# Top-32 attention with an MLP behind it: masks as a parametric ReLU on ScalarE, the mean taken from x by GpSimd, the first eight units turned one step sooner

## The chip, the cores and the metric

The kernel runs on one core of one Trainium2 chip. The metric is the device time of one execution in microseconds (us); less is better. The engines are called as in the profile: PE (TensorE matmul), PEld (its weight loads), DVE (VectorE), ACT (ScalarE), POOL (GpSimd), SP (SyncE, which issues DMAs). All arithmetic is float32.

## What is computed

```python
# q, k, v: (8, 8, 576, 64)      w_ch1: (512, 2048)   w_ch2: (2048, 512)   g_ln: (512,)
scores = q @ k.transpose(0, 1, 3, 2) / sqrt(64)
kth    = the 32nd largest of each row
scores = where(scores >= kth, scores, -1e9)
attn   = softmax(scores)                       # denominator + 1e-9
x      = (attn @ v), heads side by side        # (8, 576, 512)

mu, var = mean and variance of each row of x
xn  = (x - mu) / sqrt(var + 1e-6) * g_ln
out = x + relu(xn @ w_ch1) @ w_ch2
```

`1 / sqrt(var + 1e-6)` is positive, so it can be applied after the ReLU and the second product, and the kernel does so. Both weights come as float64 and are turned to float32 on the chip, piece by piece (32 pieces of 128 x 512).

## The kernel before

The work is cut into 160 **units**: for a batch `b` and a pair of heads `hp`, one tile of 128 query rows (two heads, so two score tiles of 128 x 576), or the **rest** of 64 rows of both heads (one tile of 128 x 576). Batch 0 has units 0 to 7 (query tiles 0 and 1 of the four pairs), 8 to 15 (tiles 2 and 3) and 16 to 19 (the rests). Units of one job form a **group**, for which the product with v is made at once. When the fourth pair of a group of tiles is done, the rows of x are complete, and a **block** of 2 or 3 tiles of 128 rows goes to the MLP.

One step `n` of the main loop works on several units at once: scores of unit n+1, selection of the 32 largest of unit n, mask of unit n-1, exponential and transposition of unit n-2, product with v of the group that ended at n-3.

```python
def select(u, i):                       # four rounds, i = 0..3
    nt = range(len(u.tiles))
    ...
    for t in nt:
        nc.vector.max(m[:, t, :], u.cur[t])            # the 8 largest
    if i < TOP_K // 8 - 1:
        for t in nt:
            ...
            nc.vector.match_replace(u.wk[t][:], m[:, t, :], u.cur[t], LOWEST)
    ...
    u.thr = m                           # thr[:, t, 7] is the 32nd largest

def prepare(u):
    ...
    if u.shared:                        # units 0..15, beside the weights
        ...
        nc.scalar.activation(u.e[:, 0], u.sc[:, 0], AF.Sign, bias=u.less[:])
        nc.scalar.activation(u.e[:, 0], u.e[:, 0], AF.Relu, scale=MASKED)
    else:
        nc.gpsimd.tensor_scalar_mul(u.bias[:, 0:nt], u.top[:, 0:nt, 0], -scale)

def mask(u, t):
    e, sc = u.e[:, t], u.sc[:, t]
    if u.shared and t == 0:
        nc.gpsimd.tensor_tensor(e, sc, e, ALU.subtract)
    else:
        nc.gpsimd.tensor_scalar(e, sc, u.thr[:, t, 7:8], MASKED, ALU.is_lt, ALU.mult)
        nc.gpsimd.tensor_tensor(e, e, sc, ALU.add)
```

A weight piece goes through `fetch` (DMA), `split` (three ACT ops and a clamp on POOL), `shift` (DVE) and `join` (two POOL ops), spread over three steps. Before, two pieces are split in each of the steps 0 to 15. The first weight is centred, so that the mean of a row of x falls out of the product: each column has g times the weight, less the mean of that over the 512 rows.

```python
def mean_of(nb):                        # 4 matmuls for each quarter of w_ch1
    means[nb] = product("mean")
    for c in range(NC):
        nc.tensor.matmul(means[nb][:], gmat[0][:, c], w1[:, c, nb * DM : (nb + 1) * DM], ...)

def centre(nb):                         # 4 DVE ops for each quarter
    for c in range(NC):
        w = w1[:, c, nb * DM : (nb + 1) * DM]
        nc.vector.scalar_tensor_tensor(out=w, in0=w, scalar=gcol[:, c : c + 1],
                                       in1=means[nb][:], op0=ALU.mult, op1=ALU.subtract)
    centred[nb] = now[0]
```

The MLP of a block is a list of small items for PE (`todo`): transposition of x (0.44), then 64 `hidden` matmuls (0.44 for two tiles, 0.66 for three) and 16 `project` matmuls for each tile (0.875). These are the kernel's own constants in us. In each step `fill` is called eight times; each call adds a share to `owed` and takes items while they are paid for. `DVE_UNIT, DVE_REST = 10.3, 5.3`, and `pe_cost` adds what PE does for attention in that step: 1.5 for scores (1.25 for a rest), 1.0 for transpositions (0.67), 3.0 when a group's product is due.

```python
def fill():
    owed[0] = min(owed[0] + share[0], 6.0)
    while todo and owed[0] >= todo[0][1] / 2 and (not todo[0][3] or todo[0][3]()):
        pop()

def slot(n):
    if not all(map(done, ready)):       # weights not all turned yet
        return 1.2
    return max(0.0, dve_cost(n) - pe_cost(n)) / SLOTS
```

What is left in `todo` when the loop ends runs on PE at the end. A `hidden` item may run only when its quarter of `w_ch1` is done, a `project` item when its piece of `w_ch2` is.

Of the kernel before, what the change touches and what calls it, by code (L numbers as in the profile page):

```python
# [18 lines left out]
MASKED = -1.0e30  # L19
LN_EPS = 1.0e-6  # L20
J = 4
# [7 lines left out]
def kernel(  # L29
# [9 lines left out]
):  # L39

# [91 lines left out]
    class Piece:  # L132
# [49 lines left out]
        def join(self):  # L182
            size = self.size[:]
            nc.gpsimd.tensor_tensor(size, size, self.low[:].bitcast(U32), ALU.add)
            nc.gpsimd.tensor_tensor(  # L185
                self.dst, size.bitcast(FP32), self.sign[:], ALU.mult
            )
            ready[self.i] = now[0]
# [4 lines left out]
    centred = [None] * (DFF // DM)  # L193
    pieces = [Piece(i) for i in range(2 * NF)]
    gmat = [None]
    means = {}
# [3 lines left out]
    def load_gain():  # L200
        ps = turned()
        nc.tensor.transpose(ps[:, 0:NC], grow[:], ident[0:NC, 0:NC])
        nc.scalar.copy(gcol[:], ps[:, 0:NC])
        ones = hpool.tile([P, P], FP32, tag="h", name="ones")
        nc.gpsimd.memset(ones[:], 1.0)
        gmat[0] = hpool.tile([P, NC, P], FP32, tag="h", name="gmat")
        for c in range(NC):
            nc.gpsimd.tensor_scalar(
                gmat[0][:, c], ones[:], gcol[:, c : c + 1], 1.0 / DM, ALU.mult, ALU.mult
            )  # L210

    def mean_of(nb):

        means[nb] = product("mean")
        for c in range(NC):
            nc.tensor.matmul(
                means[nb][:],
                gmat[0][:, c],
                w1[:, c, nb * DM : (nb + 1) * DM],
                start=(c == 0),  # L220
                stop=(c == NC - 1),
            )

    def centre(nb):
        for c in range(NC):
            w = w1[:, c, nb * DM : (nb + 1) * DM]
            nc.vector.scalar_tensor_tensor(  # L227
                out=w, in0=w, scalar=gcol[:, c : c + 1], in1=means[nb][:],
                op0=ALU.mult, op1=ALU.subtract,
            )  # L230
        centred[nb] = now[0]
# [4 lines left out]
    for n in range(-1, 2 * NF):  # L236
        size = 0 if n < 0 else 2
        batches[n], queue = queue[:size], queue[size:]

    def weights(n, phase):  # L240

        now, before = batches.get(n, []), batches.get(n - 1, [])
        if phase == 0:
            for x in batches.get(n + 1, []):
                x.fetch()
            for x in before:
                x.shift()
            for x in now[0::2]:
                x.split()
        elif phase == 1:  # L250
            for x in before:
                x.join()
            for x in now[1::2]:
                x.split()
            for x in batches.get(n - 2, []):
                if x.i < NF and x.c == NC - 1:
                    mean_of(x.i // NC)
        elif phase == 2:
            for nb in means:
                if centred[nb] is None:  # L260
                    centre(nb)
# [67 lines left out]
    class Unit:  # L329
        def __init__(self, job, group, qt):  # L330
            self.job, self.group, self.qt = job, group, qt
            self.rest = qt == J
            self.tiles = [(0, 1)] if self.rest else [(0,), (1,)]
            self.shared = False
# [63 lines left out]
    def prepare(u):  # L398

        nt = len(u.tiles)  # L400
        u.bias = small.tile([P, 2], FP32, tag="bias", name="bias")
        u.e = epool.tile([P, 2, S], FP32, tag="e", name="e")
        if u.shared:
            u.less = small.tile([P, 1], FP32, tag="less", name="less")
            nc.scalar.mul(u.less[:], u.thr[:, 0, 7:8], -1.0)
            nc.scalar.mul(u.bias[:, 0:nt], u.top[:, 0:nt, 0], -scale)
            nc.scalar.activation(u.e[:, 0], u.sc[:, 0], AF.Sign, bias=u.less[:])
            nc.scalar.activation(u.e[:, 0], u.e[:, 0], AF.Relu, scale=MASKED)
        else:
            nc.gpsimd.tensor_scalar_mul(u.bias[:, 0:nt], u.top[:, 0:nt, 0], -scale)  # L410

    def mask(u, t):
        e, sc = u.e[:, t], u.sc[:, t]
        if u.shared and t == 0:
            nc.gpsimd.tensor_tensor(e, sc, e, ALU.subtract)
        else:
            nc.gpsimd.tensor_scalar(  # L417
                e, sc, u.thr[:, t, 7:8], MASKED, ALU.is_lt, ALU.mult
            )
            nc.gpsimd.tensor_tensor(e, e, sc, ALU.add)  # L420

    def weigh(u, t):
        g = u.group
        if g.den is None:
            g.den = denpool.tile([P, 2 * J + 1], FP32, tag="den", name="den")
        col = 2 * u.qt + t
        nc.scalar.activation(  # L427
            u.e[:, t], u.e[:, t], AF.Exp, bias=u.bias[:, t : t + 1], scale=scale,
            accum_out=g.den[:, col : col + 1],
        )  # L430
        if u.rest:
            den = g.den[:, 2 * J : 2 * J + 1]
# [6 lines left out]
        nc.scalar.activation(den, den, AF.Copy, bias=DEN_EPS)  # L439
# [115 lines left out]
    class Block:  # L555
# [7 lines left out]
        def stats(self, i):  # L563
            x = self.x[i]
            if self.mv is None:
                self.mv = small.tile([P, J, 2], FP32, tag="mv", name="mv")
                self.rstd = small.tile([P, J], FP32, tag="rstd", name="rstd")
            st = small.tile([P, 6], FP32, tag="st", name="st")
            nc.vector.bn_stats(out=st[:], in_=x)
            nc.vector.bn_aggr(out=self.mv[:, i, :], in_=st[:])  # L570

# [10 lines left out]
        def items(self):  # L582
# [38 lines left out]
            def project(i, f):  # L621
# [9 lines left out]
                if f == NF - 1:  # L631
                    o = opool.tile([P, DM], FP32, tag="o", name="o")
                    nc.scalar.mul(o[:], ps["o"][:], self.rstd[:, i : i + 1])  # L633
                    nc.gpsimd.tensor_tensor(o[:], o[:], self.x[i], ALU.add)  # L634
                    for dst, rows in self.dsts[i]:
# [10 lines left out]
                        lambda f=f: done(centred[f * P // DM]),  # L646
# [45 lines left out]
    for u in units[: max(n for n in batches if batches[n]) + 1]:  # L692
        u.shared = True
# [12 lines left out]
    for j in jobs:  # L706
        if j.hp == NHP - 1:
            b = j.b
            step = j.last + 4
# [19 lines left out]

    DVE_UNIT, DVE_REST = 10.3, 5.3  # L730
# [3 lines left out]
    for j in fresh[2:]:  # L734
        before = jobs[jobs.index(j) - 1]
        turns[min(before.first, j.first - 2)] = j

    def at(i):
        return units[i] if 0 <= i < N else None

    def pe_cost(n):
        c = 0.0
        if at(n + 1):
            c += 1.25 if at(n + 1).rest else 1.5
        if at(n - 2):
            c += 0.67 if at(n - 2).rest else 1.0
        u = at(n - 3)
        if u and u.group.last == n - 3:
            c += 3.0
        return c  # L750
# [15 lines left out]
    def slot(n):  # L766

        if not all(map(done, ready)):
            return 1.2
        return max(0.0, dve_cost(n) - pe_cost(n)) / SLOTS  # L770

    recips, rows_of = {}, {}

    def arrived(n, key, x):
        blk, i = block_of[key]
        blk.x[i] = x
        rows_of.setdefault(n + 1, []).append((blk, i))

    load(fresh[0], nc.sync, nc.scalar)
    weights(-1, 0)  # L780
    turn_heads(fresh[0])
    load(fresh[1], nc.sync, nc.scalar)
    nc.sync.dma_start(grow[:], g_ln.rearrange("(c p) -> c p", p=P))
    scores(units[0])
    turn_heads(fresh[1])
    load(fresh[2], nc.sync, nc.sync)
    for n in range(END):
# [4 lines left out]
        u, nxt, mk, ex = at(n), at(n + 1), at(n - 1), at(n - 2)  # L792
        g = at(n - 3).group if at(n - 3) and at(n - 3).group.last == n - 3 else None
# [3 lines left out]
        parts = turn(ex) if ex else []  # L797

        if ex:
# [3 lines left out]
        if n == 0:  # L803
            load_gain()
# [15 lines left out]
        if ex and len(ex.tiles) > 1:  # L820
# [13 lines left out]
        for blk, i in rows_of.pop(n, []):  # L834
            blk.stats(i)
        for blk in gives.get(n - 1, []):
            blk.std()
        if mk and len(mk.tiles) > 1:
            mask(mk, order[1])
# [14 lines left out]
        if ex and ex.group.last == n - 2 and ex.group.sums is not None:  # L854
# [6 lines left out]
        weights(n, 2)  # L861
# [4 lines left out]
        if mk and mk.job.last == n - 1:  # L866
            load_values(mk.job)
        if ex and ex.group.quick and ex.group.last == n - 2:

            g = ex.group  # L870
            values(g)
            for den in recips.pop(n + 1):
                nc.vector.reciprocal(den, den)
            place(g)
        if u:
            select(u, 3)
        if g and g.job.hp == NHP - 1:
            for qt in g.qts:
                if qt < J:
                    arrived(n, (g.job.b, qt), xs[g.job.b, qt])  # L880
        if late and late.job.hp == NHP - 1:
            r = late.job.b // 2
            arrived(n, ("r", r), rs[r])
# [34 lines left out]
```

## Time and profile before

| | |
|---|---|
| time, median of 3 | 1764.3 us (1763.01 to 1764.35) |
| span of the profiled execution | 1760.9 us |
| PE busy | 1651.3 us, 94% |
| DVE busy | 1522.1 us, 86% |
| POOL busy | 1196.2 us, 68% |
| ACT busy | 983.8 us, 56% |
| granted TensorE clock, mean | 0.976 |

How to read it: the shares are means over the span, and the span has stages. So the views that count are those by stage: the busy digits in 40 slices, and the busy time of each engine in stretches cut at the start of certain units. In a line of groups, the columns are source line, engine, operation, output and inputs, shape and count, then busy us and mean ns of one, then idle time of the engine just before and what ended it. DVE runs `select` for every unit: seven ops per tile, of 742 to 746 ns each (MAX8 and MATCH_REPLACE8). Matmuls in float32 appear as two records each.

### The profile page before, as it was taken

How to read it: one execution, taken by the hardware profiler on the slowest of the kernel's cores; microseconds unless marked ns; L12 is line 12 of the kernel's file. 1: busy time of each engine (PE TensorE's matmuls, PEld its weight loads, DVE VectorE, ACT ScalarE, POOL GpSimd, SP SyncE). 2: the span in 40 equal slices, each digit the busy share in tenths (PEclk: the TensorE clock that was granted, in tenths of full speed). 3: DMA queues.
4: the chain of work that ended last, by engine and by line, in shares of the span. 5: the costliest groups of instructions: out<-in, count | busy, mean ns of one | idle time of the engine just before them, and what ended most of it. 6: DMA issues, size and time to landing. Idle time of an engine off the chain costs nothing.

```text
span 1760.9 us, 23686 instructions
## 1 busy us (share of the span) xinstructions
PE 1651.3 (94%) x7433; PEld 1005.2 (57%) x7433; DVE 1522.1 (86%) x3160; ACT 983.8 (56%) x2621; POOL 1196.2 (68%) x882
## 2 busy tenths in 40 slices
PE   3668879999899999999999999999999999999998
PEld 1335446666555575655546666575555757575564
DVE  7998779999999999999999999999999999960000
ACT  5676856565655566557646656566555665561110
POOL 5886887777776787777777687687768868760000
PEclk9868899999999999999999999999999999999999
DMA  5432312101210022002111121012201210000000
GB/s 136 124 86 67 90 37 54 40 20 21 50 31 7 26 47 47 20 20 47 21 42 25 21 53 28 26 24 45 39 12 26 43 34 20 20 20 12 0 18 12
DMA packets 249348, 66.70 MB, mean 38 GB/s; under 512 B 240516, under 2 KB 240520, under 8 KB 249224
## 3 DMA queue, kind: packets, MB, share of 16 engines
q1 hardware_dynamic: 244488, 64.61, 16.2%
q10 hardware_dynamic: 4736, 0.59, 0.3%
q8 instruction: 59, 0.97, 0.2%
q14 instruction: 65, 0.53, 0.1%
HBM read 55.71 MB, written 9.44 MB: 37 GB/s over the span
## 4 chain that ended last, share of the span: by engine, by line
PE 45%; DVE 33%; issue 14%; POOL 5%; ACT 2%; DMA 1%; DVEq 0%; POOLq 0%; SPq 0%; ACTq 0%
DVE m L387 17%; PE hps L607 15%; PE ops L624 14%; DVE wk L392 13%; PE scps L370 6%; PE tp L451 4%; PE av L504 4%; POOL e L417 2%; PE av L511 1%; DVE size L178 1%; POOL e L420 1%; DVE qT L325 1%; DVE kT L325 1%; DVE w L227 1%; ACT e L427 1%
## 5 line engine op out<-in xcount | busy, mean ns | idle before, releaser
L417 POOL TENSOR_SCALAR e<-sc,m 128x576 f32<-128x576 f32 x272 | 604.1, 2221 | 208.9 <-DVE m L387 137.9
L387 DVE MAX8 m<-wk 128x8 f32<-128x576 f32 x864 | 612.6, 746 | 3.7
L607 PE MATMUL hps<-xT,w 128*128 128x256 f32 (+1 forms) x2048 | 545.0, 411 | 7.4 <-ACT xT L599 6.2
L624 PE MATMUL ops<-w,h 128*128 128x512 f32 x1152 | 542.2, 601 | 7.1 <-POOL w L185 7.1
L607 PEld LDWEIGHTS hps<-xT,w 128*128 128x128 f32 x2048 | 374.0, 191 | 113.7 <-issue 18.8
L392 DVE MATCH_REPLACE8 wk<-m,wk 128x576 f32<-128x576 f32 x576 | 423.8, 742 | 0.0
L420 POOL TENSOR_TENSOR e<-e,sc 128x576 f32<-128x576 f32 x272 | 383.4, 1410 | 22.7
L624 PEld LDWEIGHTS ops<-w,h 128*128 128x128 f32 x1152 | 202.6, 191 | 195.5 <-issue 180.4
L370 PE MATMUL scps<-kT,qT 64*128 64x288 f32 (+3 forms) x1344 | 236.4, 439 | 26.5 <-DVE qT L325 19.9
L351 ACT COPY sc<-scps 128x288 f32<-128x288 f32 x576 | 198.5, 417 | 91.4 <-PE scps L370 83.1
L451 PE MATMUL tp<-ident,e 128*128 128x128 f32 x1152 | 180.9, 281 | 56.1 <-ACT e L427 56.0
L427 ACT ACTIVATE e<-e,bias 128x576 f32<-128x576 f32 x288 | 227.4, 790 | 8.6 <-POOL e L420 4.0
L451 PEld LDWEIGHTS tp<-ident,e 128*128 128x128 f32 x1152 | 143.8, 144 | 144.8 <-ACT e L427 70.9
L370 PEld LDWEIGHTS scps<-kT,qT 64*128 64x128 f32 (+1 forms) x1344 | 134.6, 181 | 136.1 <-issue 49.1
L392 DVE MATCH_REPLACE8 wk<-m,sc 128x576 f32<-128x576 f32 x288 | 211.9, 742 | 0.0
L387 DVE MAX8 m<-sc 128x8 f32<-128x576 f32 x288 | 203.4, 743 | 9.2 <-ACT sc L351 9.1
L619 ACT ACTIVATE h<-hps 128x256 f32<-128x256 f32 (+1 forms) x256 | 104.8, 412 | 185.9 <-PE hps L607 185.0
L634 POOL TENSOR_TENSOR o<-o,x 128x512 f32<-128x512 f32 x32 | 40.7, 1271 | 245.8 <-ACT o L633 224.9
L463 ACT COPY pt<-tp 128x512 f32<-128x512 f32 x256 | 150.3, 587 | 90.0 <-PE tp L451 88.4
L504 PE MATMUL av<-pt,vb 128*64 128x256 f32 (+2 forms) x1088 | 146.0, 409 | 2.8 <-ACT pt L463 2.0
L504 PEld LDWEIGHTS av<-pt,vb 128*64 128x64 f32 x1088 | 72.5, 140 | 68.6 <-issue 24.5
L516 ACT COPY oT<-av 128x256 f32<-128x256 f32 (+2 forms) x68 | 26.2, 386 | 108.7 <-PE av L511 108.7
(71 smaller groups left out, 1038.6 us busy)
## 6 DMA issues: line engine op xcount, KB each, us to landing
vb<-in_v_dram SPq DMA_DIRECT2D x136, 128.0 KB, 2.4
raw<-in_moe_w_ch_dram SPq DMA_DIRECT2D x32, 512.0 KB, 4.2
kin<-in_k_dram SPq DMA_DIRECT2D x128, 72.0 KB, 2.4
qin<-in_q_dram SPq DMA_DIRECT2D x120, 72.0 KB, 2.5
out_dram<-o SPq DMA_DIRECT2D x32, 256.0 KB, 2.1
ends<-in_v_dram SPq DMA_DIRECT2D x136, 16.0 KB, 2.1
dr<-den SPq DMA_DIRECT2D x64, 0.2 KB, 1.7
out_dram<-o SPq DMA_DIRECT2D x8, 128.0 KB, 2.3
```

The costliest lines, as they stand in the source:

```text
L351: nc.scalar.copy(u.sc[:, t, s * HALF : (s + 1) * HALF], made[s][t][:, 0:HALF])
L370: nc.tensor.matmul(ps[i * R : i * R + ql, o : o + width], qT[r, q0 : q0 + ql], kT[r, k0 : k0 + width], start=True, stop=True,)
L387: nc.vector.max(m[:, t, :], u.cur[t])
L392: nc.vector.match_replace(u.wk[t][:], m[:, t, :], u.cur[t], LOWEST)
L417: nc.gpsimd.tensor_scalar(e, sc, u.thr[:, t, 7:8], MASKED, ALU.is_lt, ALU.mult)
L420: nc.gpsimd.tensor_tensor(e, e, sc, ALU.add)
L427: nc.scalar.activation(u.e[:, t], u.e[:, t], AF.Exp, bias=u.bias[:, t : t + 1], scale=scale, accum_out=g.den[:, col : col + 1],)
L451: nc.tensor.transpose(ps[:, c * P : (c + 1) * P], u.e[:, t, c * P + t * R : (c + 1) * P + t * R], ident[:],)
L463: nc.scalar.copy(g.pt[:, t * J : (t + 1) * J, q0 : q0 + P], ps[:].rearrange("p (c n) -> p c n", n=P),)
L504: nc.tensor.matmul(av[h * D : (h + 1) * D, 0 : g.nq], vb[:, h * J + c, :], g.pt[:, h * J + c, 0 : g.nq], start=(c == 0), stop=False,)
L607: nc.tensor.matmul(ps["h"][:, 0:N], w1[:, c, f * P : (f + 1) * P], xT[0][:, c, 0:N], start=(c == 0), stop=(c == NC - 1),)
L624: nc.tensor.matmul(ps["o"][:], hT[f][:, i * P : (i + 1) * P], w2[:, f, :], start=(f == 0), stop=(f == NF - 1),)
```

## The change

It does five things.

- **Masks on ScalarE.** One ACTIVATE makes `prelu(thr - score)` with slope 2^-90: a kept score gives a tiny negative number, a masked one a positive one. The exponential then takes it with the scale `-scale / SLOPE` and the bias `scale * (thr - top)`: the kept scores come back, the masked ones fall to zero. GpSimd makes no masks any more; it makes the bias in two small ops.
- **Mean from x.** `x` has its mean subtracted in place by GpSimd, which frees the first weight from centring (no `mean_of`, no `centre`); GpSimd multiplies its pieces by the gain instead. At the end the mean comes back as the bias of the op that scales the output.
- **Weights one step sooner.** Two pieces are split before step 0, so the batches run from -1 to 14. The shift stands later in the step.
- **First eight units one step sooner.** Units 0 to 7 have mask, exponential and transposition in one step, n-1. So the first block goes to the MLP at step 9 instead of 10.
- **Even pacing.** The share of 1.2 while weights are turned is gone; all steps use the difference of DVE and PE costs.

Besides, the second transposition of q and k moves from before the loop into step 0, and a small copy on ACT stands ahead of the first scores. It is for freeing GpSimd and DVE beside the weights, and for letting the MLP start sooner and run evenly.

```diff
-MASKED = -1.0e30
+SLOPE = 2.0**-90
...
         def join(self):
             size = self.size[:]
             nc.gpsimd.tensor_tensor(size, size, self.low[:].bitcast(U32), ALU.add)
-            nc.gpsimd.tensor_tensor(
-                self.dst, size.bitcast(FP32), self.sign[:], ALU.mult
-            )
+            size = size.bitcast(FP32)
+            if self.i < NF:
+                gain = gcol[:, self.c : self.c + 1].to_broadcast([P, DM])
+                nc.gpsimd.tensor_tensor(size, size, gain, ALU.mult)
+            nc.gpsimd.tensor_tensor(self.dst, size, self.sign[:], ALU.mult)
...
-    for n in range(-1, 2 * NF):
-        size = 0 if n < 0 else 2
-        batches[n], queue = queue[:size], queue[size:]
+    for n in range(-1, NF - 1):
+        batches[n], queue = queue[:2], queue[2:]
...
-            for x in before:
-                x.shift()
             for x in now[0::2]:
                 x.split()
         elif phase == 1:
             for x in before:
+                x.shift()
+            for x in before:
                 x.join()
...
     def mask(u, t):
-        ...
+        nc.scalar.activation(
+            u.e[:, t], u.sc[:, t], AF.Prelu, bias=u.thr[:, t, 7:8], scale=-1.0, alpha=SLOPE
+        )
...
-            u.e[:, t], u.e[:, t], AF.Exp, bias=u.bias[:, t : t + 1], scale=scale,
+            u.e[:, t], u.e[:, t], AF.Exp, bias=u.bias[:, t : t + 1], scale=-scale / SLOPE,
...
             nc.vector.bn_aggr(out=self.mv[:, i, :], in_=st[:])
+            nc.gpsimd.tensor_scalar_sub(x, x, self.mv[:, i, 0:1])
...
-                    nc.scalar.mul(o[:], ps["o"][:], self.rstd[:, i : i + 1])
+                    nc.scalar.activation(
+                        o[:], ps["o"][:], AF.Identity,
+                        bias=self.mv[:, i, 0:1], scale=self.rstd[:, i : i + 1],
+                    )
...
-            step = j.last + 4
+            step = j.last + (3 if j.last < EARLY else 4)
...
-    for j in fresh[2:]:
+    for j in fresh[1:]:
         before = jobs[jobs.index(j) - 1]
         turns[min(before.first, j.first - 2)] = j
...
     def slot(n):
 
-        if not all(map(done, ready)):
-            return 1.2
         return max(0.0, dve_cost(n) - pe_cost(n)) / SLOTS
...
         if mk:
-
             prepare(mk)
-            order = list(range(len(mk.tiles)))
-            if mk.shared:
-                order.reverse()
-            mask(mk, order[0])
+        if early:
+            for t in range(2):
+                mask(ex, t)
+                weigh(ex, t)
...
         weights(n, 1)
         fill()
-        fill()
+        if mk and not early:
+            mask(mk, 0)
         if g:
             place(g)
         if late:
             place_rest(late.job.b, late.job.hp)
+        fill()
+        if mk and len(mk.tiles) > 1 and not early:
+            mask(mk, 1)
         fill()
```

More of the change, by code (lines that the diff above doesn't have):

```diff
@@ L192 @@
     ready = [None] * (2 * NF)
-    centred = [None] * (DFF // DM)
     pieces = [Piece(i) for i in range(2 * NF)]
-    gmat = [None]
-    means = {}
     grow = hpool.tile([NC, P], FP32, tag="h", name="grow")
@@ L203, in load_gain @@
         nc.scalar.copy(gcol[:], ps[:, 0:NC])
[L204 to L231, printed above, removed]
     batches = {}
     queue = list(pieces)
-    for n in range(-1, 2 * NF):
-        size = 0 if n < 0 else 2
-        batches[n], queue = queue[:size], queue[size:]
+    for n in range(-1, NF - 1):
+        batches[n], queue = queue[:2], queue[2:]
     def weights(n, phase):
@@ L254, in weights @@
                 x.split()
[L255 to L261, printed above, removed]
     todo = []
@@ L333, in __init__ @@
             self.tiles = [(0, 1)] if self.rest else [(0,), (1,)]
-            self.shared = False
     class Group:
@@ L402, in prepare @@
         u.e = epool.tile([P, 2, S], FP32, tag="e", name="e")
[L403 to L410, printed above, removed]
-    def mask(u, t):
[L413 to L420, printed above, removed]
+        b = u.bias[:, 0:nt]
+        nc.gpsimd.tensor_tensor(b, u.thr[:, 0:nt, 7], u.top[:, 0:nt, 0], ALU.subtract)
+        nc.gpsimd.tensor_scalar_mul(b, b, scale)
+    def mask(u, t):
+        nc.scalar.activation(
+            u.e[:, t], u.sc[:, t], AF.Prelu, bias=u.thr[:, t, 7:8], scale=-1.0, alpha=SLOPE
+        )
     def weigh(u, t):
@@ L645, in items @@
                         lambda f=f, c=c: hidden(f, c),
-                        lambda f=f: done(centred[f * P // DM]),
+                        lambda f=f, c=c: done(ready[f * P // DM * NC + c]),
                     )
@@ L690 @@
             fresh.append(j)
-    for u in units[: max(n for n in batches if batches[n]) + 1]:
-        u.shared = True
+    EARLY = jobs[NHP].first
     full = slice(0, P)
@@ L728, with at, after @@
     SLOTS = 8
+    def at(i):
+        return units[i] if 0 <= i < N else None
+    def after(n):
+        turned = at(n - 1) if n - 1 < EARLY else at(n - 2) if n - 2 >= EARLY else None
+        last = at(n - 2) if n - 2 < EARLY else at(n - 3) if n - 3 >= EARLY else None
+        return turned, last.group if last and last is last.group.units[-1] else None
     DVE_UNIT, DVE_REST = 10.3, 5.3
     turns = {}
-    for j in fresh[2:]:
+    for j in fresh[1:]:
         before = jobs[jobs.index(j) - 1]
         turns[min(before.first, j.first - 2)] = j
-    def at(i):
-        return units[i] if 0 <= i < N else None
     def pe_cost(n):
@@ L744, in pe_cost @@
             c += 1.25 if at(n + 1).rest else 1.5
[L745 to L748, printed above, removed]
+        ex, g = after(n)
+        if ex:
+            c += 0.67 if ex.rest else 1.0
+        if g:
             c += 3.0
@@ L766, in slot, with arrived @@
     def slot(n):
-        if not all(map(done, ready)):
-            return 1.2
         return max(0.0, dve_cost(n) - pe_cost(n)) / SLOTS
-    recips, rows_of = {}, {}
-    def arrived(n, key, x):
+    recips = {}
+    def arrived(key, x):
         blk, i = block_of[key]
         blk.x[i] = x
-        rows_of.setdefault(n + 1, []).append((blk, i))
+        blk.stats(i)
     load(fresh[0], nc.sync, nc.scalar)
-    weights(-1, 0)
[L781 to L786, printed above, removed]
+    nc.scalar.copy(gcol[:, 0:1], eps[:])
+    for x in batches[-1]:
+        x.fetch()
+    turn_heads(fresh[0])
+    nc.sync.dma_start(grow[:], g_ln.rearrange("(c p) -> c p", p=P))
+    load(fresh[1], nc.sync, nc.scalar)
+    scores(units[0])
+    load_gain()
+    weights(-1, 0)
+    weights(-1, 1)
     for n in range(END):
@@ L791 @@
         share[0] = slot(n)
-        u, nxt, mk, ex = at(n), at(n + 1), at(n - 1), at(n - 2)
-        g = at(n - 3).group if at(n - 3) and at(n - 3).group.last == n - 3 else None
+        u, nxt, mk = at(n), at(n + 1), at(n - 1)
+        ex, g = after(n)
         g = g if g and not g.quick else None
@@ L797 @@
         parts = turn(ex) if ex else []
-        if ex:
+        early = ex is not None and n - 1 < EARLY
+        last = ex and ex is ex.group.units[-1]
+        if ex and not early:
             weigh(ex, 0)
@@ L802 @@
             scores(nxt)
-        if n == 0:
-            load_gain()
         if g:
@@ L813 @@
             prepare(mk)
-            order = list(range(len(mk.tiles)))
-            if mk.shared:
-                order.reverse()
-            mask(mk, order[0])
+        if early:
+            for t in range(2):
+                mask(ex, t)
+                weigh(ex, t)
         weights(n, 0)
         fill()
-        if ex and len(ex.tiles) > 1:
+        if ex and len(ex.tiles) > 1 and not early:
             weigh(ex, 1)
@@ L833 @@
                 load(fresh[later], nc.sync, nc.sync)
-        for blk, i in rows_of.pop(n, []):
-            blk.stats(i)
         for blk in gives.get(n - 1, []):
             blk.std()
-        if mk and len(mk.tiles) > 1:
-            mask(mk, order[1])
         weights(n, 1)
         fill()
-        fill()
+        if mk and not early:
+            mask(mk, 0)
         if g:
@@ L853 @@
             blk.inverse()
-        if ex and ex.group.last == n - 2 and ex.group.sums is not None:
+        if last and ex.group.sums is not None:
             recips.setdefault(n + 1, []).append(ex.group.sums)
@@ L860 @@
             recips.setdefault(n + 1, []).append(den)
-        weights(n, 2)
         fill()
@@ L865 @@
         fill()
[L866 to L871, printed above, removed]
+        for x in (u if n < EARLY else None, mk if n > EARLY else None):
+            if x and x is units[x.job.last]:
+                load_values(x.job)
+        quick = ex.group if last and ex.group.quick else None
+        if quick:
+            values(quick)
             for den in recips.pop(n + 1):
                 nc.vector.reciprocal(den, den)
-            place(g)
+            place(quick)
         if u:
             select(u, 3)
[L877 to L880, printed above, removed]
+        for x in (g, quick):
+            if x and x.job.hp == NHP - 1:
+                for qt in x.qts:
+                    if qt < J:
+                        arrived((x.job.b, qt), xs[x.job.b, qt])
         if late and late.job.hp == NHP - 1:
             r = late.job.b // 2
-            arrived(n, ("r", r), rs[r])
+            arrived(("r", r), rs[r])
         fill()
```

## The prediction

> **What bounds the kernel now.** I read the span in 40 slices first, then the busy time by stage, then the waits of the early stage, then the groups.
>
> The slices (one digit per 44 us):
>
> ```profile
> PE   3668879999899999999999999999999999999998
> DVE  7998779999999999999999999999999999960000
> POOL 5886887777776787777777687687768868760000
> PEclk9868899999999999999999999999999999999999
> ```
>
> Three stages are to be seen. In the first six slices no engine is full throughout. From the seventh on PE and DVE are both at 9. DVE ends in slice 36 and PE goes on alone: the MLP that is left over.
>
> The same by stage. Columns: stretch, its length, then busy us (and instructions) of PE, PEld, DVE, ACT, POOL, then granted clock, DMA share and GB/s. I cut where units begin on DVE: unit 1 at 24.4 us, unit 10 at 143.6, unit 16 at 225.8, unit 20 at 261.0 (the starts of the first-round MAX8 `m<-sc` in the timeline).
>
> ```profile
> 24.40:143.60 119.20, 67.73 (x248) 37.23 (x248) 119.20 (x223) 81.97 (x201) 103.46 (x81) 0.81 0.36 101
> 143.60:225.80 82.20, 70.00 (x321) 46.82 (x321) 67.66 (x141) 65.95 (x162) 64.91 (x50) 0.88 0.24 73
> 225.80:261.00 35.20, 27.93 (x137) 14.90 (x133) 26.14 (x52) 16.39 (x50) 27.79 (x23) 0.90 0.19 38
> 261.00:1571.00 1310.00, 1290.12 (x6101) 793.71 (x6099) 1294.70 (x2720) 776.85 (x2110) 982.88 (x703) 0.99 0.15 31
> 1571.00:1761.00 190.00, 184.25 (x602) 105.94 (x600) 1.98 (x6) 33.59 (x78) 13.41 (x10) 1.00 0.03 10
> ```
>
> Up to unit 10 DVE is busy 119.2 of 119.2 us, so it alone sets the step. From 143.6 to 261.0 it is idle 14.5 + 9.1 = 23.6 us and no other engine is full. From 261 to 1571 DVE is busy 98.8% and PE 98.5%: DVE sets the step, and the MLP is dosed so that PE just keeps up. The last 190 us are PE alone.
>
> What DVE waits for before 261 us (columns: waiter, what it waited for, total, times, longest):
>
> ```profile
> DVE size L178 <- POOL size L175: 13.9, 5, 4.3
> DVE kT L325 <- DMA kin<-in_k_dram: 12.0, 2, 6.5
> DVE den L810 <- ACT den L439: 5.2, 2, 2.8
> DVE m L387 <- ACT sc L351: 3.4, 1, 3.4
> ```
>
> The shift of a weight piece waits on GpSimd, 13.9 us; the second load of keys at the start holds DVE too (5.5 of the 12.0 us; the other 6.5 are the first load, which nobody can skip). The groups that the change touches:
>
> ```profile
> L417 POOL TENSOR_SCALAR e<-sc,m 128x576 f32<-128x576 f32 x272 | 604.1, 2221 | 208.9 <-DVE m L387 137.9
> L420 POOL TENSOR_TENSOR e<-e,sc 128x576 f32<-128x576 f32 x272 | 383.4, 1410 | 22.7
> ...
> L216 PE MATMUL mean<-w,gmat 128*128 128x512 f32 x32 | 17.6, 702 | 0.0
> ...
> L407 ACT ACTIVATE e<-sc,less 128x576 f32<-128x576 f32 x16 | 12.4, 775 | 0.0
> L227 DVE SCALAR_TENSOR_TENSOR w<-w,gcol,mean 128x512 f32<-128x512 f32 x16 | 10.8, 734 | 0.0
> ```
>
> The masks are the largest thing on POOL, 604.1 + 383.4 us, but POOL is 75% busy in the long stage and nobody waits long for it there.
>
> **What the Trainium skill says.** "ScalarE: Activation LUTs", What ACT_TABLE_LOAD costs: an ACTIVATE with a pointer bias takes about 280 ns + 0.833 ns per element, an estimate of 760 ns for 576; the trace has 775 ns for the Sign that has such a bias, so 0.78 us is my price of one Prelu. The same section gives a table load about 1283 ns; the trace has 16 of 1283 ns before the square roots. "ScalarE activation tables: per-element evaluation and per-set limits", Table sets and What a function is: two functions in one set need no switch. Neither page names the set of Prelu; I take it to lie beside Exp as Sign, Relu, Abs and Copy do here, which alternate with Exp without a load. "GPSIMD Engine Reference", 3.1: a two-input op runs at about 2.6 cycles per element, an estimate of 1.11 us for 512 before its overhead; the trace has 1286 ns for `w<-size,sign`, my price for the gain multiply.
>
> **The change, part by part.**
>
> 1. *Masks.* POOL loses 272 x (2.22 + 1.41) = 987 us and the 16 x 1.51 us subtractions. ACT gains 288 x 0.78 = 225 us and loses the 16 Sign and Relu (12.4 + 10.9), about 202 us net. In the long stage ACT goes from 777 to about 777 + 252 x 0.78 = 974 of 1310 us, 74%. It stays below DVE. Gain on the path there: at most the 15.3 us that DVE is idle, and that idleness is not put down to POOL. I expect none, and a small loss, because ACT also empties PSUM in order: about +4 us.
>
> 2. *Mean from x.* The 32 mean matmuls (17.6 us) leave PE in a stage where PE is 57% busy: nothing. The 16 centring ops (10.8 us, 4 x 2.63 in the chain) leave DVE where DVE is full: **10.5 us off the path**. In their place POOL multiplies 16 pieces by the gain, 16 x 1.28 = 20 us, and subtracts the mean 36 times; both off the path, since POOL in an early step falls from about 11.5 us (3.6 + 1.5 masks, 6.3 weights) to about 9. A first transposition of x must now wait for that subtraction; it bites only where the backlog is empty, the first few blocks.
>
> 3. *POOL out of the way of the weights.* The 13.9 us of DVE waiting for the clamp should go, most of the 5.2 for the denominators too. I count **10 us**, keeping some for new waits: an early ACT step (9 us of 13 now, about 10 with the Relus of the MLP) gets fuller.
>
> 4. *Start.* The second transposition no longer stands ahead of the first MAX8, and the first table load is pulled forward. First MAX8 at 14.8 now; scores are ready to be copied by about 10, so about 11. The transposition (1.5 us) and now a shift (2 us) move into step 0, but the weights also finish one step sooner (one shift pair fewer later). **About 3 us.**
>
> 5. *First eight units one step sooner, pacing.* The first block is given at step 9 instead of 10. I followed `todo`, `owed` and `fill` through both programs with their own cost constants. Before: 1.2 x 8 = 9.6 us of MLP a step up to step 16; after: 4.8 to 8.05, (10.3 - PE cost). The projections of the first block are gated by the second weights in both, so at step 20 the backlog is 58.7 us before and 57.8 after, at the last unit 120.4 in both, and after the last step 155.4 in both. **So this part brings nothing by itself**: the tail keeps its 190 us. What it can bring is that PE does not stall in 143 to 200 us; I count 0 to 4 us, taken as 1.
>
> Sum to unit 20: 10.5 + 10 + 3 + 1 = about 24 us, so unit 20 starts at about 237 instead of 261. A check from the other side: DVE is busy 225.4 of these 261 us; less 10.8 for the centring and with about 9.5 us of idleness at the start the floor is 224, and the four rest units (16 to 19) bring PE about 27 us of work against 24 of DVE, so 3 and some waits are added: 235 to 240. From there everything shifts: 1764.3 - 24 + 4 = **1744 us**.
>
> **Rivals.**
>
> *ACT becomes the bound.* For it: all evacuations, both halves of the softmax and now the masks stand in one in-order queue; in the rest steps (5.3 us of DVE) slack is nil: at 926.3 us the score copies start, at 927.3 DVE takes them up. If each of 28 rest steps lost 1 us, 28 us would be given back, and the time would be about 1768. Against it: 74% on average, and an ACT mask needs a threshold that DVE finished at the end of the step before, with PE and ACT some 3 us behind DVE.
>
> *Prelu needs its own table.* Then two loads of 1.28 us per unit: 160 x 2.6 = 410 us on ACT, which would be over 1200 of 1310 us in the long stage; time well above 1800. I give it 2%.
>
> *POOL was the hidden bound.* It holds nearly a third of the span in masks. If the 15.3 us of DVE idleness in the long stage and its PE companions came from it, another 10 us go: 1730. Against: no POOL line among the waits of DVE after 261 us (only 5.7 us for score copies).
>
> *The whole early stage becomes PE- or ACT-paced.* Then unit 20 starts at about 250 and the time is 1755 or more.
>
> **Range and chances.** Early gain 12 to 33 us, long stage -8 to +20, tail unchanged: 1728 to 1766. Faster by 2% means below 1729.7, which needs nearly the whole early floor and a gain in the long stage: 0.11. Slower by 2% needs a table load or a real ACT bound: 0.05.
>
> **What would show it.** Right: no L227 or L216 successor; DVE `size` waiting for POOL below 4 us; the first MAX8 near 11 us; unit 20 on DVE at 232 to 245; 31 or 32 table loads as now; ACT about 1180 us and POOL about 260 to 300 busy; 185 to 195 us of PE alone at the end; DVE still above 98% between. Wrong: score copies from ACT as the main wait of DVE in the long stage, PE waiting there for `pt` or `h` by more than 20 us, or a tail of another length, which would mean that my following of the backlog missed something.

## The result and the profile after

The changed kernel takes **1807.6 us** (median of 4) against 1764.0: ratio 1.025, 95% interval 1.0218 to 1.0282. It is slower, and 42 us above the upper end of the predicted range.

The 40 slices of the page of the changed kernel (busy tenths; its execution took 1802.7 us, 5 us less than the median, so that differences of stages come out some us below those of medians):

```profile
PE   3669989999799999999999999999999999999998
DVE  7869899999888999989998999899998999870000
ACT  6768876675565776667757776687667766682111
POOL 4665510100100111010111010111001010101000
```

POOL is nearly empty, as intended. But DVE, which was at 9 from slice 7 to slice 35, now falls to 8 again and again.

The same by stage, cut at the same events as for the kernel before (unit 1, unit 10, unit 16, unit 20, last selection). Columns: stretch, length, busy us (and instructions) of PE, PEld, DVE, ACT, POOL, clock, DMA share, GB/s:

```profile
22.90:143.60 120.70, 73.90 (x247) 41.53 (x248) 100.40 (x211) 79.66 (x183) 79.91 (x91) 0.69 0.38 100
143.60:207.70 64.10, 59.94 (x289) 39.65 (x287) 63.09 (x136) 59.62 (x139) 39.90 (x48) 0.97 0.28 80
207.70:238.00 30.30, 28.43 (x172) 16.18 (x170) 24.67 (x50) 22.50 (x65) 7.35 (x13) 1.00 0.29 59
238.00:1611.00 1373.00, 1329.84 (x6084) 804.84 (x6082) 1296.30 (x2719) 936.11 (x2356) 145.48 (x369) 0.98 0.15 30
1611.00:1801.00 190.00, 182.86 (x594) 104.44 (x593) 2.24 (x8) 34.89 (x78) 12.36 (x11) 0.99 0.03 10
```

Unit 20 starts at 238.0 instead of 261.0: 23 us won. The tail is 190 us as before. Everything is lost in between: **1373 us instead of 1310** for the same 140 units, with DVE just as busy (1296 and 1295 us). So DVE stands idle for 61 us more (76.7 against 15.3). What for, from the waits of DVE in this stage (total, times, longest), in the kernel before and then in the changed one:

```profile
DVE m L387 <- ACT sc L351: 5.7, 5, 2.1
```

```profile
DVE st L526 <- ACT x L477: 37.6, 10, 5.5
DVE m L354 <- ACT sc L318: 33.1, 14, 4.8
```

Both are waits for ScalarE, though ScalarE is busy only 936 of 1373 us, 68%. The first is the row statistics, which this change also moved: from the middle of the next step to the end of the step in which x is placed. So there were two suspects at once: the place of the statistics (theory A in what follows) and the masks crowding ScalarE's queue (theory B). A third was the subtraction of the mean on the way to PE (theory C).

### The profile page after: what moved, and what is told of

Same layout as the page of the kernel before. It is cut to its first block, busy times and chain, and to the rows that moved or that the text cites. A ratio compares the mean times of both kernels' runs of the same rounds, so it can differ in the third digit from the quotient of the medians.

```text
span 1800.9 us, 23419 instructions
## 1 busy us (share of the span) xinstructions
PE 1682.3 (93%) x7401; PEld 1011.0 (56%) x7401; DVE 1500.0 (83%) x3144; ACT 1145.3 (64%) x2846; POOL 292.0 (16%) x545
## 4 chain that ended last, share of the span: by engine, by line
PE 54%; DVE 20%; issue 11%; ACT 9%; POOL 5%; DMA 0%; POOLq 0%; DVEq 0%; SPq 0%; ACTq 0%
PE ops L582 19%; PE hps L565 17%; DVE m L354 10%; DVE wk L359 8%; PE scps L337 7%; PE av L461 5%; PE tp L408 4%; ACT e L375 2%; ACT pt L420 2%; PE av L468 2%; ACT e L384 1%; ACT x L477 1%; POOL w L194 1%; POOL size L189 1%; POOL size L193 1%
## 5 line engine op out<-in xcount | busy, mean ns | idle before, releaser
L565 PE MATMUL hps<-xT,w 128*128 128x256 f32 (+1 forms) x2048 | 551.5, 414 | 2.0 <-ACT xT L557 1.4
L337 PE MATMUL scps<-kT,qT 64*128 64x288 f32 (+3 forms) x1344 | 265.2, 442 | 45.2 <-ACT pt L420 17.3
L408 PEld LDWEIGHTS tp<-ident,e 128*128 128x128 f32 x1152 | 145.8, 146 | 143.6 <-ACT e L384 69.5
L375 ACT ACTIVATE e<-sc,m 128x576 f32<-128x576 f32 x288 | 220.4, 779 | 0.9 <-DVE m L354 0.9
L371 POOL TENSOR_TENSOR bias<-m,m 128x2 f32<-128x2 f32 (+1 forms) x160 | 31.1, 194 | 688.1 <-DVE m L354 639.2
```

Of the source, the lines that this page charges most:

```text
L337: nc.tensor.matmul(ps[i * R : i * R + ql, o : o + width], qT[r, q0 : q0 + ql], kT[r, k0 : k0 + width], start=True, stop=True,)
L375: nc.scalar.activation(u.e[:, t], u.sc[:, t], AF.Prelu, bias=u.thr[:, t, 7:8], scale=-1.0, alpha=SLOPE)
L408: nc.tensor.transpose(ps[:, c * P : (c + 1) * P], u.e[:, t, c * P + t * R : (c + 1) * P + t * R], ident[:],)
L565: nc.tensor.matmul(ps["h"][:, 0:N], w1[:, c, f * P : (f + 1) * P], xT[0][:, c, 0:N], start=(c == 0), stop=(c == NC - 1),)
```

## The experiments

All are timed beside the kernel before, and the ratios are to it. "Last selection" below is the start of the last MAX8 pair in the profile, "long stage" the time from unit 20 to there.

**Which part costs it.** In e1 the statistics are issued later:

```diff
         for den in recips.pop(n, []):
             nc.vector.reciprocal(den, den)
         if mk:
             prepare(mk)
+        for blk, i in rows_of.pop(n, []):     # x placed in step n-1
+            blk.stats(i)
```

> The changed kernel, but the row statistics (and the subtraction of the mean) are issued after the first selection round of the following step instead of at the end of the step in which x is placed. Theory A (statistics in line: DVE stands at the end of the step and waits for ScalarE to write x, 37.6 us in all after unit 20): those waits vanish and nothing takes their place, about 1770 us. Theory B (crowded ScalarE queue: masks delay whatever PSUM evacuation stands behind them, and DVE or PE would be late anyway): the wait only moves to the score copies, 1790 to 1805 us. Theory C (mean chain: PE waits for the subtraction before it can transpose x): no better or worse, 1805 to 1815 us.

Measured: 1811.7 us, ratio 1.0279 [1.0264, 1.0294]. Theory A falls: the wait for x shrinks from 37.6 to 20.1 us (in a window from 262 us on), and the wait for score copies grows to 58.9. DVE met a late ScalarE elsewhere. The time lies in the range of theory C too; e2 settles that.

In e2 the masks go back to GpSimd from unit 16 on:

```diff
     def mask(u, t):
+        if u.on_pool:                         # units 16..159
+            nc.gpsimd.tensor_scalar(e, sc, u.thr[:, t, 7:8], MASKED, ALU.is_lt, ALU.mult)
+            nc.gpsimd.tensor_tensor(e, e, sc, ALU.add)
+            return
...
```

The bias and the places of these masks are those of the kernel before as well.

> The changed kernel, but units 16 to 159 have their masks on GpSimd with the two ops and at the place of the kernel before; the first sixteen units keep the Prelu. Statistics stay at the end of the step. Theory A: DVE still waits for x at the end of the step, since the exponentials and copies on ScalarE stay; 1790 to 1800 us. Theory B: ScalarE falls from 70% to about 58% in the long stage, x and the score copies come sooner, both DVE waits (37.6 and 33.1 us) shrink to under 10 us each; about 1755 us. Theory C: unchanged within 5 us, 1803 to 1812.

Measured: **1751.1 us**, 0.9934 [0.9919, 0.9949]. That gives back 56 us and is faster than the kernel before. Both DVE waits fall to 13 to 14 us. The subtraction is still there, so theory C is not the main cause.

> Both edits together: statistics after the first selection round of the next step, masks of units 16 to 159 on GpSimd. If A and B between them hold the whole 63 us lost in the long stage, this runs at the time first predicted, 1740 to 1748 us. Theory A alone: as with the later statistics only, about 1770. Theory B alone: as with the GpSimd masks only, about 1755. Theory C: above 1790.

Measured: 1757.7 us, 0.9971 [0.9959, 0.9982]. The later statistics cost 6 us here. PE waits longer for the subtraction that follows them: 16.9 us against 10.6 in e2, from 262 us on.

e4 is the other way round: the kernel before with the Prelu masks alone, from unit 16 on, at the changed kernel's places.

> The kernel before, with one part of the change alone: the masks of units 16 to 159 as Prelu on ScalarE, at the places where the changed kernel has them; statistics, centring, pacing as before. Theory A: 1760 to 1768 us, since its statistics stand in the following step and never wait. Theory B: 1785 to 1800 us, with score copies as DVE's wait. Theory C: 1760 to 1768.

Measured: 1818.4 us, 1.0311 [1.0294, 1.0328], 55 us slower, with 53.6 us of DVE waiting for score copies. Theory B's number was too small, its direction right: the masks on ScalarE are the loss, with or without the rest. And the place of the statistics by itself, in the kernel before (`rows_of.setdefault(n + 1, ...)` replaced by `blk.stats(i)`):

> The kernel before with one edit: the row statistics at the end of the step in which x is placed, where the changed kernel has them (masks on GpSimd, no subtraction of the mean). If the place of the statistics costs DVE time by itself, 13 blocks at some 4 us, 1790 to 1810 us. If the waits seen there were only ScalarE being late because of the masks, 1762 to 1772 us; I expect this one.

Measured: 1768.3 us, 1.0025 [1.0014, 1.0035]: 5 us. No subtraction hangs on the statistics there, so this does not contradict e3.

**Why 0.78 us ops on an engine that is 68% busy cost 54 us.** One step of the changed kernel, first ScalarE, from its timeline (start, duration, line, what; in brackets the idle time before and its cause):

```profile
660.99 1.49 ACT L318 COPY sc<-scps 128x288 f32<-128x288 f32 x4 [0.84 <-PE scps L337]
663.99 0.37 ACT L473 COPY oT<-av 128x256 f32<-128x256 f32 x1 [1.51 <-PE av L468]
664.26 0.78 ACT L384 ACTIVATE e<-e,bias 128x576 f32<-128x576 f32 x1
...
665.50 0.78 ACT L375 ACTIVATE e<-sc,m 128x576 f32<-128x576 f32 x1
666.17 0.92 ACT L477 ACTIVATE x<-xo,den 128x64 f32<-128x64 f32 x4
666.96 0.80 ACT L375 ACTIVATE e<-sc,m 128x576 f32<-128x576 f32 x1
667.62 0.61 ACT L420 COPY pt<-tp 128x512 f32<-128x512 f32 x1
```

and PE with its weight loads in the same microseconds:

```profile
665.88 2.02 PE L337 MATMUL scps<-kT,qT 64*128 64x288 f32 x6
668.28 0.75 PE L337 MATMUL scps<-kT,qT 64*128 64x288 f32 x2 [0.39 <-ACT pt L420]
```

```profile
666.74 0.70 PEld L337 LDWEIGHTS scps<-kT,qT 64*128 64x128 f32 x4 [0.57 <-ACT x L477]
668.28 0.29 PEld L337 LDWEIGHTS scps<-kT,qT 64*128 64x128 f32 x2 [0.84 <-ACT pt L420]
```

The scores need four of the five banks of their pool in PSUM (the memory that matmuls write to). Other banks still hold the turned output (`xo`) and transposed scores (`tp`), and ScalarE empties them only after the two masks (`e<-sc,m`, L375) that stand ahead. So scores that take 1.24 us almost six microseconds earlier (660.21, x8) take from 665.88 to 669.03, 3.15 us. PE is full in this stage, so the time that it stands is lost. Only 0.5 us of it shows as a gap between matmul records: each record keeps its length, and what shrinks is their overlap. The score matmuls of full units in the whole run, before and after, have the same number and nearly the same mean, but cover 28 us more:

```profile
L370 PE MATMUL scps<-kT,qT 64*128 64x288 f32 x1024 | 196.6, 459 | 25.3 <-DVE qT L325 19.9 <-ACT pt L463 2.8 <-ACT x L520 2.2
```

```profile
L337 PE MATMUL scps<-kT,qT 64*128 64x288 f32 x1024 | 225.1, 463 | 42.9 <-ACT pt L420 17.3 <-DVE qT L293 16.2 <-ACT x L477 4.0
```

The waits of PE's weight loads over the whole run, first before, then after:

```profile
PEld scps L370 <- ACT pt L463: 10.4, 33, 1.4
PEld scps L370 <- ACT x L520: 6.6, 6, 1.7
```

```profile
PEld scps L337 <- ACT pt L420: 37.9, 43, 1.7
PEld scps L337 <- ACT x L477: 27.9, 38, 2.4
```

The timeline also shows where ScalarE had time to spare: 1.51 us ahead of `oT<-av`. Two experiments follow from that reading. e6 keeps every op and moves the two masks into that gap (and the two small bias ops on GpSimd with them):

```diff
         if nxt:
             scores(nxt)
+        if mk and not early:
+            prepare(mk)
+            for t in range(len(mk.tiles)):
+                mask(mk, t)
         if g:
             values(g)
...
```

> The changed kernel with both masks of a unit moved in ScalarE's order: right behind the score copies and ahead of the copy of the product with v, where ScalarE stood idle for 1.5 us in the changed kernel when a group was due. Same ops, same load of ScalarE. If the loss is one of place (masks stand ahead of PSUM evacuations that PE waits for), most of it comes back: 1755 to 1775 us. If it is one of load, 1800 to 1815 us.

Measured: **1753.9 us**, 0.9941 [0.9926, 0.9955]. The same load of ScalarE (1145 us busy in both) at another place: 54 us less. The waits of the loads fall to 18.7 us for `pt` and 8.2 for `x`. It is the place. What the masks still cost there is little: e2, without them from unit 16 on, is 2.8 us faster than e6.

e8 leaves the masks where they are and gives the pool a sixth bank, taken from the MLP (`pool("ps", 6)`, `pool("mmps", 2)`):

> The changed kernel with PSUM cut otherwise: six banks for scores, transpositions and products with v instead of five, two for the MLP instead of three. In the changed kernel PE's score matmuls wait more for ScalarE's copies out of transposed tiles and of x than before (37.9 and 27.9 us against 10.4 and 6.6). If the late evacuation hurts by holding that pool, 1760 to 1785 us. If PE and DVE lose elsewhere, or the MLP now suffers from two banks, 1800 us or more.

Measured: 1762.1 us, 0.9996 [0.9987, 1.0004]: 45 us less. The waits of the loads for `pt` fall from 37.9 to 1.4 us, those for `x` only from 27.9 to 23.2. So the banks held behind the masks are most of the mechanism. e9 issues each mask from unit 16 on twice:

> The changed kernel with every Prelu of units 16 to 159 issued twice (the second writes the same values again): 256 - 16 and some more ops of 0.78 us on ScalarE, 193 us. If the loss goes with ScalarE's occupancy at that place, another 45 to 70 us: 1850 to 1880. If it came from the first mask waiting for DVE's threshold, the second costs little: below 1820.

Measured: 1916.5 us, 1.0865 [1.0847, 1.0884]: 109 us more for 181 us more of ScalarE work, with ScalarE 75% busy in the long stage (1112 of 1480 us). The waits of PE's matmuls themselves, 10.9 and 1.7 us in the changed kernel between 238 and 1620 us, grow to:

```profile
PE scps L337 <- ACT pt L421: 33.8, 30, 1.2
PE scps L337 <- ACT x L478: 26.3, 27, 2.5
```

My 45 to 70 us was too low: the second op at the same place costs about twice the first.

**The clock beside the waits.** The records of the granted clock read 1.0 or 0.5 in all these traces. In the step shown above, 0.2 us after the late scores end, the clock goes to 0.5 for 3.4 us (stretch, length, busy us and instructions of PE, PEld, DVE, ACT, POOL, clock, DMA share, GB/s):

```profile
669.30:672.70 3.40, 3.40 (x10) 2.70 (x9) 3.40 (x9) 2.30 (x8) 2.00 (x4) 0.50 0.01 2
```

In the long stage such stretches make 13.7 us in the kernel before (3 of them), 54.6 us in the changed one (11), 30.7 us in e6 (6) and 174.1 us in e9 (31). Nine of the 11 and 30 of the 31 begin within 1.7 us of the end of a wait of PE's score matmuls. An `ops` matmul record of 592 ns takes up to 1220 ns in them. If half the clock means half the work of PE, these sums give an estimate of 20 us for the clock's part in the loss of the changed kernel, and of 60 us in the further 109 of e9. Not every wait is followed by such a stretch, and no run separates the two, so it is not shown that the waits bring it on.

Both remedies together:

> The changed kernel with both remedies: masks right behind the score copies, and six banks of PSUM for attention, two for the MLP. If both remedies cure the same thing (PE's scores waiting for banks that ScalarE empties late), the sum is little better than the better one: 1745 to 1755 us. If they cure different things, the 54 and the 45 us add in part: below 1740.

Measured: 1749.9 us, 0.9918 [0.9903, 0.9933]; only 4 us on top of the moved masks, so for the most part they cure the same thing.

**The first eight units.** The prediction said that turning them sooner brings nothing. e11 is e6 with `EARLY = 0`:

> As e6_gap (masks behind the score copies), but the first eight units are not turned one step sooner; the first block is given at step 10 as before the change. The prediction held that this part brings nothing by itself, since the backlog of the MLP at step 20 is the same: 1749 to 1758 us against 1753.9. If the earlier start counts, a step or so is lost: 1762 or more.

Measured: **1737.7 us**, 0.9851 [0.9836, 0.9865]. The early turn does not bring nothing, it costs 16 us. The waits of DVE in the first 240 us, with the early turn (e6) and then without (e11):

```profile
DVE size L183 <- POOL size L180: 12.9, 9, 2.8
DVE st L526 <- ACT x L477: 10.5, 2, 9.1
```

```profile
DVE m L354 <- ACT sc L318: 3.9, 2, 3.2
DVE st L526 <- ACT x L477: 3.4, 2, 2.2
DVE size L183 <- POOL size L180: 2.7, 3, 1.7
```

What ScalarE's exponentials and masks wait for in the same 240 us, e6 and then e11:

```profile
ACT e L384 <- POOL bias L372: 13.6, 5, 4.1
```

```profile
ACT e L375 <- DVE m L354: 11.5, 9, 3.3
```

In e6 an exponential follows its selection within one step, and five times it waits for its bias from GpSimd. The bias stands there behind the joins and a clamp of the weights: in one step the last join ends at 91.26 us, the clamp at 91.84 and the bias at 92.38, and the exponential, idle for 2.12 us, starts at 92.41. The splits of the weights stand behind it on ScalarE and come late, and with them the next clamp and the shift on DVE; GpSimd's clamps wait 67.6 us for the splits in e6 and 37.7 in e11. Unit 10 starts at 143.6 us in the kernel before and in the changed one, at 143.4 in e6 and at 122.5 in e11: the early turn takes back all that the other parts win up to there. Unit 20 starts at 218.1 us in e11 and at 236.1 in e6. That this ring of waits is all of the 16 us is not shown; the early turn as its cause is. In the changed kernel itself, the same single edit:

> The changed kernel with the one edit of e11: first eight units at the ordinary place, masks where the change put them. If the loss of early turning (18 us up to unit 20) and the loss of the mask's place (54 us) are separate, 1789 to 1794 us. If early turning only hurts in company of the moved masks, 1800 or more.

Measured: 1794.2 us, 1.0179 [1.0143, 1.0214]: 13 us less, with executions from 1788.7 to 1801.3 us. The place of the masks still costs 57 us here (e16 against e11), so the two losses stand apart.

**What is left.** Blocks and statistics one step later, to take both waits out of the chain of the mean:

> As e6_gap, but the statistics stand after the first selection round of the next step, and each block is given to the MLP one step later, so that neither DVE waits for x nor PE for the subtraction of the mean. If the rest of the loss (unit 20 to the last selection is 1327 us there against 1310 in the kernel before) is this chain, 1738 to 1748 us. If not, within 4 us of 1753.9, or worse because a block one step later leaves PE without MLP work while the backlog is empty.

Measured: 1769.4 us, 1.003 [1.002, 1.004]: 15.5 us worse than e6. The last selection came 5 us later and PE's time alone at the end grew by about 10, with 653 matmul records there instead of 604: a block given later leaves PE without MLP work while its list is empty, and that work comes back at the end.

> All three: masks behind the score copies, six and two banks, statistics and blocks one step later. As e12_gap_late_blocks or up to 6 us better, 1735 to 1746 us, if the chain of the mean is what is left; else as e10_gap_banks.

Measured: 1762.7 us, 0.9989 [0.9981, 0.9996]; the banks win 7 us of it back, no more.

> As e11_gap_no_early, but the subtraction of the mean by GpSimd is left out (36 ops of 1.57 us), so the MLP gets x with its mean: a measurement of what this chain costs, not a usable kernel. If PE's wait for the subtraction (about 10 us of PE waits for transposing x after unit 20) is what keeps the long stage some 20 us above the kernel before, 1722 to 1730 us. If the cost lies in the place of the statistics and in ScalarE, 1735 to 1738.

Measured: 1727.6 us, 0.9798 [0.9782, 0.9813]. Left out is the subtraction, so what is computed is not the reference; as a measurement, the subtraction between the statistics and the transposition costs **10 us** (1737.7 to 1727.6).

> As e11_gap_no_early with six banks for attention and two for the MLP. The banks gave 4 us on top of the moved masks (1753.9 to 1749.9), so 1733 us if that adds; 1738 or more if PE no longer waits for banks at all.

Measured: **1730.6 us**, 0.9824 [0.9804, 0.9844]. This is the best full version: the change with its masks moved into the gap, six and two banks, and without the early turn. It is faster than both kernels, by 1.8% and 4.3%.

| kernel | time, us | unit 20 | last selection | long stage |
|---|---|---|---|---|
| before | 1764.0 | 261.0 | 1567.3 | 1306 |
| changed | 1807.6 | 238.0 | 1609.8 | 1372 |
| e2, masks on GpSimd | 1751.1 | 237.9 | 1559.9 | 1322 |
| e6, masks in the gap | 1753.9 | 236.1 | 1562.0 | 1326 |
| e11, e6 without early turn | 1737.7 | 218.1 | 1547.2 | 1329 |
| e14, e11 with six banks | 1730.6 | 221.5 | 1537.3 | 1316 |

## Why the prediction was wrong, point by point

**Part 1, the masks: the step that failed.** "A small loss, because ACT also empties PSUM in order: about +4 us" was the term. The long stage lost 63 us, and moving the masks alone gives back 54 us of the time (46 of the stage in the profiles: 1372 to 1326). Statistics and subtraction hold part of the rest: e15 gives the subtraction 10. The price of the load itself was about right: e2 and e6, with the masks off and on ScalarE, differ by 2.8 us. What the term left out is the place. The sum of ScalarE's work was near (1145 us busy for about 1180, 936 in the long stage for 974, 0.779 us for a Prelu, 32 table loads as before), and it did stay below DVE; that the loss must then be small didn't follow. Load says whether an engine can keep up over a stage, not how late one particular op comes. The rival "ACT becomes the bound" named the queue and put it at 28 us, in the rest steps only; the waits lie at full units as well, and no bound of ScalarE is needed. The wait was with PE's score matmuls and their banks, which I had not looked at, since the profile of before shows little of it (10.4 and 6.6 us). Both signs that the prediction named for being wrong appeared: score copies among DVE's main waits (33.1 us) and PE's side waiting for `pt` (37.9 us on the loads).

**Part 2, mean from x.** The centring is gone from DVE as said, but the changed kernel won nothing by it up to unit 10, which starts at 143.6 us in both: DVE, full there before, stands 20.3 of 120.7 us. "It bites only where the backlog is empty" was right in kind (PE waits for the subtraction a few times after unit 20) but I gave it no time; e15 measures 10 us. The ops take 1.57 us each.

**Part 3, GpSimd out of the way.** The 10 us were to come from DVE's waits for the clamp. Those stayed: 12.4 us instead of 13.9, since the early turn made the splits late. e11 shows that they can go (2.7 us).

**Part 4, start.** First MAX8 at 11.1 us, predicted about 11.

**Part 5, early turn and pacing.** The backlog argument held for the tail: 190 us in both. But "brings nothing by itself" looked only at PE's list and not at what ScalarE then has to wait for: it costs 16 us (e6 to e11).

**The sum to unit 20** came out at 237 predicted and 238.0 measured by luck, from errors that cancel: the early turn cost what the shift and the other parts won beyond the sum. DVE's floor of 224 was wrong too, as e11's 218.1 shows. I took 10.8 us off DVE's 225.4 for the centring; it is busy 201.4 us in the changed kernel. The other 13 us are the shift of the weights, 32 ops that got faster without being changed themselves. In the groups, before and then after:

```profile
L178 DVE TENSOR_SCALAR size<-size 128x512 uint32<-128x512 uint32 x32 | 29.6, 954 | 13.9 <-POOL size L175 13.9
```

```profile
L183 DVE TENSOR_SCALAR size<-size 128x512 uint32<-128x512 uint32 x32 | 16.1, 525 | 12.4 <-POOL size L180 12.4
```

## What to carry to other kernels

When work moves to an engine that empties PSUM in order, ask not how busy it will be but what stands behind each new op, which banks stay full meanwhile, and who wants them next; put the op where that engine waits anyway. A part that "brings nothing" must be followed through every engine it reorders, not only the one it was made for. And a sum that comes out right says little about its terms: cut the stages and check each. Look at the granted clock beside each wait of PE as well, since the wait may not be all that is lost.

## What the runs showed of the hardware

The shift on DVE takes 0.38 us at its fastest in the changed kernel and up to 1.51 us in the kernel before; its mean falls from 0.954 to 0.525 us with the same op and the same data, when GpSimd loses its masks and the shift stands later in the step. The Trainium skill, "GPSIMD Engine Reference", 1. Specifications, says that GpSimd's SBUF interfaces are shared with VectorE, with contention for VectorE instructions in a 2-port perf mode or with two SBUF inputs. The trace agrees that there is contention: in the kernel before, 24 of the 32 shifts begin while a GpSimd op is running, take 0.83 to 1.51 us, and each ends 0.28 to 0.29 us after that op; the other eight take 0.40 to 0.43 us. In which mode the shift runs, no run shows. MAX8 and MATCH_REPLACE8 (746 and 742 ns in both kernels) don't mind.

A GpSimd op with a scalar for each partition was slow here: 1.57 us for the subtraction on 128 x 512 against 0.63 us for the clamp with two constants on the same shape. The arithmetic differs too, so it is not shown that the scalar is the reason.
